# One product moved behind two others, two PSUM rings swapped, and attention steps issued earlier in a fused attention and MLP kernel

## The chip, the core and the metric

The kernel runs on one core of a Trainium2 chip. The metric is device time in microseconds of one execution. The median of three runs before the change is 495.05 us (492.89 to 496.14).

## The reference

x is 2048 x 512 (float32). It is normalised by row; from the normalised rows come a dilated local attention and an MLP that gates it.

```python
x = A_x
xn = _layernorm(x)                                    # 2048 x 512
q, k, v = split(xn @ wqkv)                            # 512 x 1536; 32 heads of 16
idx = pos[:, None] - 2 * arange(8)                    # 8 keys, 2 rows apart
logits = einsum(q, k[idx]) * 16 ** -0.5               # idx < 0: -1e9
s = einsum(softmax(logits), v[idx]) @ wo              # 512 x 512
h = relu(xn @ w1 + b1) ** 2                           # 512 x 1792
g = silu(h @ w2 + b2)                                 # 1792 x 512
out = x + s * g
```

## The kernel before, in words

**Products in three passes.** Each float32 operand is split into a rounded high part and the rest, the low part. A product runs over high x high, high x low and low x high, so a 128 x 512 result over a depth of 512 takes 12 matmuls of 128 x 512, and one over a depth of 256 takes 6. ScalarE writes high parts (`highx`, `sum_high`, `high`), VectorE or GpSimd subtract to get low parts (`lowx`, `sum_low`, `low`, `lowh`).

**Phase 1: q, k and v** (main loop from L787). The 2048 rows are 16 tiles of 128. Tiles are taken in pairs a, b = a + 1. Pairs 0 and 2 compute q, k, v with 12 matmuls each (`qkv`). The six pairs a = 4, 6, ..., 14 go through `seven(a)` (L571): with sums and differences of the two tiles and of the weights, q and k of both tiles take seven products of 6 matmuls where eight would be needed, and v two products of 12. Its work on TensorE, in the order before, for pairs 4 to 12:

1. X, first product, into a new bank X; ScalarE then copies X into a bank Y (`A.activation(Y, X, AF.Copy)`);
2. v of tile a (`qkv(a, 2)`);
3. the second product on X, after which ScalarE copies X out as q of tile a;
4. the tail product of the pair before (`last`, L647), on that pair's bank Z, after which ScalarE copies Z out as q of its tile b;
5. v of tile b;
6. a product on Y, which ScalarE copies into a bank Z; then products on U, on Z and again on Y. VectorE adds Z and Y to U's copy (the two `V.tensor_add` into `sk_`, "stg" in the trace), which gives k.

In pair 14 v of tile b stood at the end, before the tail product, and two first products of the MLP, `up(0, 0)` and `up(0, 1)`, followed.

The third and sixth matmul of a product read the low part. The products on U, Z and Y read `ss`, the sums of two tiles: `sum_x` forms them on VectorE and GpSimd one pair ahead, `sum_high` rounds them on ScalarE, and `sum_low` subtracts one half on VectorE and the other on GpSimd. Tile t + 2 is transposed by VectorE (`trans`, L474), its high part written by ScalarE and its low part by VectorE (`lowx`).

**PSUM.** Eight banks in three rings: psA with four banks (X, v of a, v of b, U), psH with two (Y and Z of a pair, later `ph`), psT with two (the transposes, later the output product). A new tile of a ring waits until the tile that had its bank has been read for the last time.

**Attention** is a generator (L239) that issues steps on VectorE: for each of eight units of 256 rows four steps q x k (a multiplication of 128 x 2048 and a reduction), the softmax, and four steps attention x v (the same two operations). They are put between the other VectorE work by `pump(margin)` (L366). It keeps two planned clocks, of TensorE and VectorE, and issues steps as long as VectorE's planned clock, with the next step's cost, stays within TensorE's planned clock plus the margin: -500 ns without an argument, `LATE` = 3000 ns, or 500. The price of a matmul is 227 ns, that of a VectorE operation its elements / 0.96 + 170 ns. `not_before` moves VectorE's clock forward where an operation must wait for another engine. Loads of q, k and v for a unit are issued from ScalarE's queue when the planned clock has passed a due time, which `defer` holds (L231).

TensorE, VectorE, ScalarE and GpSimd keep the order in which the program issues; DMAs on SP may be reordered against the program.

**Phase 2: the MLP** (from L896) runs over four chunks c of 512 rows and 14 blocks f of 128 hidden columns: `up(c, f)` (12 matmuls into `ph` of psH; ScalarE applies relu and two squares, VectorE's `lowh(f)` the low part), then `down` of block f - 2 (12 matmuls into four banks `pb` of psA). `up(c, f)` takes the bank of `up(c, f - 2)`, which is free when `lowh(f - 2)` has read it. In chunks 1 to 3 five of the fourteen low parts are on GpSimd. In chunk 0 the weights arrive: `load_w(f)` loads w1 and w2 of block f into two pieces of SBUF, `next_w()` splits them (two ScalarE operations, two on GpSimd) and, from block 3 on, issues the load of block f + 2, which waits until GpSimd has read the pieces. The output products of a chunk (`pw`) and the gate run between blocks; the last two tiles of the last chunk need the last attention step, its store to DRAM (so) and its load (oq).

Of the kernel before, what the change touches and what calls it, by code (L numbers as in the profile page):

```python
# [10 lines left out]
AF = mybir.ActivationFunctionType  # L11
# [29 lines left out]
SEVEN = range(4, 15, 2)  # L41
# [10 lines left out]
MATMUL, TRANSPOSE, DVE_FIXED, SLACK, LATE, ROOM0, ROOM = 227, 150, 170, 500, 3000, 500, 3500  # L52
# [5 lines left out]
def body(ctx: ExitStack, tc: tile.TileContext, x, wqkv, wo, w1, b1, w2, b2, out):  # L58
# [32 lines left out]
    PE, V, A, G = Ordered(nc.tensor, "PE"), Ordered(nc.vector, "V"), Ordered(nc.scalar), Ordered(nc.gpsimd)  # L91
# [15 lines left out]
    def psA(name):  # L107
        return psum.tile([P, 512], F32, name=name, tag="acc", bufs=4)

    def psH(name):  # L110
        return psum.tile([P, 512], F32, name=name, tag="h", bufs=2)
# [38 lines left out]
    def buffer(name, i):  # L150
        return wts.tile([P, 2, 2, 512], FR, name=name, tag=f"b{i}")


    wq = [buffer(f"wq{i}", i) for i in range(6)]
# [84 lines left out]
    def attention():  # L239
# [5 lines left out]
        def qk(u, s):  # L245
# [11 lines left out]
                out=L[:, i0 * 8:(i0 + 2) * 8, :].rearrange("p m w -> p w m"),  # L257
                in_=pr.rearrange("p w (g d) -> p w g d", d=HD), axis=AX.X, op=OP.add)

# [106 lines left out]
    def pump(margin=-SLACK):  # L366

        limit = clock["PE"] + margin
        flush(clock["PE"])
        while True:  # L370
            if coming[0] is None:
                coming[0] = next(stream, None)
            if coming[0] is None or clock["V"] + coming[0] > limit:
                break
            coming[0] = next(stream, None)
        if coming[0] is None:
            not_before(limit)
# [4 lines left out]
    def load_w(f):  # L382
        if f in (1, 2):
            r1, r2 = (px.tile([P, D], F32, name=f"{n}{f}", tag="x", bufs=4) for n in ("w1r", "w2r"))
        else:
            r1, r2 = (piece(f"{n}{f}") for n in ("w1r", "w2r"))
        dma(r1.rearrange("p (k c) -> p k c", c=P), w1[:, f * P:(f + 1) * P].rearrange("(k p) c -> p k c", p=P))
        dma(r2, w2[f * P:(f + 1) * P, :])
        raws[f] = r1, r2

    def next_w():

        f = len(w12)
        if f < NF:
            w12[f] = buffer(f"w{f}", HOME[f]) if f in HOME else p2.tile([P, 2, 2, 512], FR, name=f"w{f}")
            for i, r in enumerate(raws.pop(f)):
                split(w12[f][:, 0, i], w12[f][:, 1, i], r, G)
            if 2 < f < NF - 2:
                load_w(f + 2)


    NT = S // P
# [71 lines left out]
    def trans(t, aside=False):  # L474
        place(t)
        pTs[t] = piece(f"xs{t}") if t % 2 and t - 1 in SEVEN else psT(f"pxT{t}")
        if t < TURN:
            for kt in range(KT):
                PE.transpose(pTs[t][:, kt * P:(kt + 1) * P], xn[t][:, kt * P:(kt + 1) * P], ident)
            seen[t] = clock["PE"] + 800  # L480
        else:

            V.transpose(out=pTs[t].rearrange("p (k n b) -> p b k n", k=KT, b=4),
                        in_=xb[t // 2 * 2][:, :, t % 2].rearrange("p b (k c) -> p b k c", k=KT))
            seen[t] = clock["V"] + 800
        if not aside:
            highx(t)
# [4 lines left out]
    def lowx(t):  # L492
        not_before(seen.pop(t))
        V.tensor_sub(xt[t][:, 1], pTs[t].rearrange("p (k n) -> p k n", k=KT), xt[t][:, 0].bitcast(F32))
        if t not in SEVEN and t - 1 not in SEVEN:
            pTs.pop(t)
# [18 lines left out]
    def sum_high(a):  # L515
        ss[a] = [pss.tile([P, 2, 2, 2, P], FR, name=f"ss{a}_{i}", tag="ss", bufs=2) for i in range(2)]
        for t, d in zip(sums[a], ss[a]):
            A.activation(d[:, :, 0], four(t), AF.Copy)
# [7 lines left out]
    def qkv(t, s, between=None, late=False):  # L526

        ps = (psH if t < 2 and s == 2 else psA)(f"pq{t}_{s}")
        order = [(kt, a, b) for kt in range(KT) for a, b in PASSES]
        if late:  # L530
            order.sort(key=lambda o: o[1])
        for n, (kt, a, b) in enumerate(order):
            PE.matmul(ps, xt[t][:, a, kt], wq[2 * s + kt // 2][:, b, kt % 2, :], start=n == 0, stop=n == 11)
            if between and n == 5:
                between()
        evacuate(t, s, ps)
# [34 lines left out]
    def seven(a):  # L571

        b = a + 1
        for s in (2, 0, 1):
            stgs[s] = pstg.tile([P, 4, 2, P], F32, name=f"stg{a}_{s}", tag="stg", bufs=5)
        sq_, sk_ = stgs[0], stgs[1]

        def x(t, h):
            return lambda p, k: xt[t][:, p, 2 * h + k]

        def s(i):
            return lambda p, k: ss[a][i // 2][:, i % 2, p, k]

        def product(ps, left, w, start=False, stop=False):
            n = 0
            for k in range(2):
                for p, r in PASSES:
                    PE.matmul(ps, left(p, k), w[:, r, k], start=start and n == 0, stop=stop and n == 5,
                              skip_group_check=True)
                    n += 1  # L590

        def groups(ps):
            return ps.rearrange("p (g c) -> p g c", g=4)

        X = psA(f"X{a}")
        product(X, x(a, 0), wq[0], start=True)
        Y = psH(f"Y{a}")
        A.activation(Y, X, AF.Copy)
        if a == SEVEN[0]:
            sum_high(a)  # L600
        more = a + 2 < NT
        if not more:
            sum_high(a)
        first_norm(a)
        second_norm(a)
        pump(LATE)
        qkv(a, 2)
        if more and a > SEVEN[0]:
            sum_high(a)
        pump(LATE)  # L610
        product(X, x(a, 1), wq[1], stop=True)
        A.activation(sq_[:, :, 0], groups(X), AF.Copy, scale=0.25)
        while tail:
            tail.pop()()
        sum_low(a)
        if more:
            trans(a + 2)
            pump(LATE)
            qkv(b, 2)
            lowx(a + 2)  # L620
            trans(b + 2, True)
        else:
            load_w(3)
        pump(LATE)
        product(Y, s(1), tw[T2])
        Z = psH(f"Z{a}")
        A.activation(Z, Y, AF.Copy)
        if more:
            highx(b + 2)
        else:  # L630
            next_w()
        U = psA(f"U{a}")
        product(U, s(0), tw[T1], start=True, stop=True)
        A.activation(sk_[:, :, 0], groups(U), AF.Copy)
        if more:
            lowx(b + 2)
            sum_x(a + 2)
            next_stats(a)
        pump(500)
        product(Z, s(2), tw[T3])  # L640
        product(Y, s(3), wq[3], stop=True)
        pump(500)
        V.tensor_add(sk_[:, :, 1], groups(Z), sk_[:, :, 0])
        V.tensor_add(sk_[:, :, 0], groups(Y), sk_[:, :, 0])
        store(a, 1, sk_)

        def last():  # L647
            product(Z, x(b, 1), tw[T4], stop=True)
            A.activation(sq_[:, :, 1], groups(Z), AF.Copy, scale=0.25)
            store(a, 0, sq_)  # L650

        tail.append(last)
        if not more:
            pump(LATE)
            qkv(b, 2, next_w)
            load_w(4)
            tail.pop()()
            pump(LATE)
            up(0, 0)
            next_w()  # L660
            pump()
            up(0, 1)
            lowh(0)
            pump()

    def load_xT(c):
        xT[c] = xTa.tile([P, TPC, 2, KT, P], FR, name=f"xU{c}", tag="xT")
# [2 lines left out]

    hs = {}

    def up(c, f):
        ph = psH(f"ph{c}_{f}")
        n = 0
        for kt in range(KT):
            for a, b in PASSES:
                PE.matmul(ph.rearrange("p (j n) -> p j n", n=P), w12[f][:, a, 0, kt * P:(kt + 1) * P],
                          xT[c][:, :, b, kt, :], start=n == 0, stop=n == 11)
                n += 1  # L680
        if f == NF - 1 and c + 1 < NCH:
            load_xT(c + 1)
        h = hpool.tile([P, 2, 512], FR, name=f"h{c}_{f}", tag="h", bufs=3)
        A.activation(ph, ph, AF.Relu, bias=b1t[:, f:f + 1])
        A.activation(h[:, 0], ph, AF.Square)
        aside = c > 0 and f in ASIDE
        if aside:
            r, ph = ph, p2.tile([P, 512], F32, name=f"sq{c}_{f}", tag="sq", bufs=2)
        else:
            r = ph  # L690
        A.activation(ph, r, AF.Square)
        hs[f] = h, ph, clock["PE"] + 2000, aside
# [37 lines left out]
    ps = psA("pq0_1")  # L730
# [56 lines left out]
    for a in range(2, NT, 2):  # L787
        b = a + 1
# [224 lines left out]
```

## Time and profile before

| | us |
|---|---|
| median of three runs | 495.05 |
| the profiled execution | 494.42 |
| its span | 492.3 |
| TensorE busy | 481.3 |
| VectorE busy | 438.1 |
| ScalarE busy | 228.2 |
| GpSimd busy | 168.3 |

All instructions that the kernel issues through a helper have line L87, so groups are told apart by tile: X, Y, Z, U are the banks of a pair, pq is v (in pairs 0 and 2 also q and k), xt the transposed tile, ss the sums, stg a staged result, pr and pv the products of attention, ph and pb the MLP's banks, h its hidden block, w1r and w2r raw weights. A row of the timeline gives start, duration, engine, operation, tiles, count, and in brackets the idle time before it with what ended it. DVE is VectorE, ACT is ScalarE, POOL is GpSimd, SP issues most DMAs.

### The profile page before, as it was taken

The page shows a single profiled execution, that of the slowest core. Times are in us where ns is not written, and L with a number is a line of the kernel's source. Part 1 is how long each engine was busy: PE and PEld are TensorE (multiplying, and loading weights), DVE is VectorE, ACT ScalarE, POOL GpSimd, SP SyncE. Part 2 cuts the span into 40 slices and gives each one's busy share as a digit, 9 for nine tenths or more (in the row PEclk, how much of TensorE's full clock was granted, in tenths as well). Part 3 has the DMA queues.
Part 4 walks back from the last instruction along what each step waited for, and adds up shares of the span by engine and source line. Part 5 has one row for each costly group of instructions (what it writes and reads, how often), then busy time and mean ns, then how long its engine had stood idle before and what let it go on. Part 6 is the DMA issues. An engine that isn't in the chain of part 4 may idle for free.

```text
span 492.3 us, 5906 instructions
## 1 busy us (share of the span) xinstructions
PE 481.3 (98%) x2118; PEld 395.5 (80%) x2118; DVE 438.1 (89%) x374; ACT 228.2 (46%) x403; POOL 168.3 (34%) x153
## 2 busy tenths in 40 slices
PE   8999999989899999999999999999999999999996
PEld 5888788868688888888888888888888888888885
DVE  5997889899966999999999998899999989999806
ACT  5686566734355557445612333534232453433213
POOL 1326532633676869413222322151121022411100
PEclk9999999999899999999999999999999999999999
DMA  8799788796579866191627048325520872261052
GB/s 293 228 301 329 245 255 257 268 334 242 170 235 277 249 159 225 47 328 23 224 63 221 5 169 317 70 65 194 161 94 1 330 225 65 37 195 56 1 170 85
DMA packets 48520, 88.78 MB, mean 180 GB/s; under 512 B 5372, under 2 KB 32364, under 8 KB 45676
## 3 DMA queue, kind: packets, MB, share of 16 engines
q1 hardware_dynamic: 42444, 51.72, 33.5%
q10 hardware_dynamic: 4320, 33.56, 19.2%
q0 software_dynamic: 1728, 3.15, 3.9%
q8 instruction: 16, 0.26, 0.2%
q14 instruction: 12, 0.10, 0.1%
HBM read 57.94 MB, written 27.32 MB: 173 GB/s over the span
## 4 chain that ended last, share of the span: by engine, by line
PE 80%; DMA 8%; DVE 6%; ACT 2%; SPq 2%; issue 1%; POOL 0%; ACTq 0%; DVEq 0%; POOLq 0%
PE ph L87 31%; PE pb L87 29%; PE pw L87 7%; PE pq L87 6%; DMA xb<-xn 4%; PE Z L87 2%; PE X L87 2%; PE Y L87 2%; DVE pr L87 1%; DMA so<-v 1%; SPq L472 1%; PE U L87 1%; DMA sq<-stg 1%; DVE stg L87 1%; ACT xn L87 1%
## 5 line engine op out<-in xcount | busy, mean ns | idle before, releaser
L87 PE MATMUL pb<-w,h 128*128 128x512 f32 x672 | 160.6, 389 | 0.0
L87 PEld LDWEIGHTS pb<-w,h 128*128 128x128 f32 x672 | 126.2, 188 | 26.1
L87 PE MATMUL ph<-xU,w 128*128 128x512 f32 x504 | 120.6, 389 | 0.0
L87 PEld LDWEIGHTS ph<-xU,w 128*128 128x128 f32 x504 | 94.6, 188 | 19.6
L87 ACT ACTIVATE ph<-ph,b1t 128x512 f32<-128x512 f32 x56 | 36.9, 659 | 145.1 <-PE ph L87 131.5
L87 DVE TENSOR_TENSOR pv<-v,L 128x2048 f32<-128x2048 f32 x32 | 76.8, 2399 | 0.4
L87 DVE TENSOR_TENSOR pr<-k,q 128x2048 f32<-128x2048 f32 x32 | 76.7, 2395 | 0.4
L87 DVE TENSOR_REDUCE v<-pv 128x256 f32<-128x2048 f32 x32 | 73.0, 2282 | 0.7
L87 DVE TENSOR_REDUCE L<-pr 128x128 f32<-128x2048 f32 x32 | 72.9, 2278 | 0.5
L87 POOL TENSOR_TENSOR h<-sq,h 128x512 fp32r<-128x512 f32 x15 | 25.7, 1711 | 84.2 <-ACT sq L87 75.2
L87 PE MATMUL pw<-wot,oT 128*128 128x512 f32 (+1 forms) x204 | 46.1, 377 | 0.2 <-DVE oT L87 0.2
L87 DVE TENSOR_TENSOR h<-ph,h 128x512 fp32r<-128x512 f32 x41 | 28.1, 685 | 19.7 <-ACT ph L87 19.7
L87 PEld LDWEIGHTS pw<-wot,oT 128*128 128x128 f32 x204 | 36.7, 188 | 7.7 <-DVE oT L87 0.6
L87 PE MATMUL ph<-xT,w 128*128 128x512 f32 x168 | 40.2, 390 | 0.0
L87 PEld LDWEIGHTS ph<-xT,w 128*128 128x128 f32 x168 | 31.5, 188 | 6.8 <-DVE h L87 0.3
L87 ACT ACTIVATE h<-ph 128x512 fp32r<-128x512 f32 x56 | 33.6, 600 | 2.5
L87 PE MATMUL pq<-wq,xt 128*128 128x512 f32 x144 | 34.6, 389 | 0.0
L87 PEld LDWEIGHTS pq<-wq,xt 128*128 128x128 f32 x144 | 27.0, 188 | 5.6
L87 PE MATMUL pq<-wq,xT 128*128 128x512 f32 x132 | 30.8, 392 | 0.0
L87 POOL TENSOR_TENSOR w<-w1r,w 128x512 fp32r<-128x512 f32 x14 | 25.2, 1801 | 15.6 <-ACT w L87 11.5
L87 PEld LDWEIGHTS pq<-wq,xT 128*128 128x128 f32 x132 | 24.5, 188 | 5.8 <-ACT xT L87 0.7
L87 POOL TENSOR_TENSOR L<-L,mx_None 128x512 f32<-128x512 f32 x7 | 19.5, 2791 | 27.1 <-DVE mx_None L87 27.1
(103 smaller groups left out, 533.0 us busy)
## 6 DMA issues: line engine op xcount, KB each, us to landing
k<-sk ACTq DMA_DIRECT2D x8, 1408.0 KB, 6.9
v<-sv ACTq DMA_DIRECT2D x8, 1408.0 KB, 6.8
sx<-xt SPq DMA_DIRECT2D x12, 512.0 KB, 5.2
xU<-sx ACTq DMA_DIRECT2D x6, 1024.0 KB, 6.5
x<-in_A_x SPq DMA_DIRECT2D x16, 256.0 KB, 5.5
sk<-stg SPq DMA_DIRECT2D x8, 512.0 KB, 4.4
sq<-stg SPq DMA_DIRECT2D x8, 512.0 KB, 4.1
sv<-stg SPq DMA_DIRECT2D x8, 512.0 KB, 5.4
```

What stands on the lines that cost most here:

```text
L87: return tc.keep_in_program_order(f(*a, **k))
L472: dma(xb[t][32 * a:32 * a + 32].rearrange("p b e c -> p b (e c)"), src[:, a].rearrange("p e c -> p (e c)"))
```

## The change

In `seven(a)`:

- the second product on X and the copy that follows move behind v of tile b, for all six pairs. The tail product of the pair before thus comes directly behind v of tile a;
- pair 14 gets v of tile b at the same place as the others, no longer at its end;
- `lowx(a + 2)` moves behind `trans(b + 2)`;
- `sum_high` of pair 14 moves from before v of tile a to behind it;
- one `pump(LATE)` is added ahead of the second product on X; the pump ahead of the last products on Z and Y goes from 500 to `LATE`, the one ahead of VectorE's two adds from 500 to 1500;
- behind pair 14, `up(0, 0)` and `up(0, 1)` take their banks from psT, `up(0, 0)` stands ahead of the last tail product, the split of w2 and load 4 ahead of `up(0, 0)`, the split of w3 behind `up(0, 1)`, and two pumps get `LATE`.

```diff
+        more = a + 2 < NT
         X = psA(f"X{a}")
         product(X, x(a, 0), wq[0], start=True)
         Y = psH(f"Y{a}")
         A.activation(Y, X, AF.Copy)
         if a == SEVEN[0]:
             sum_high(a)
-        more = a + 2 < NT
-        if not more:
-            sum_high(a)
         first_norm(a)
         second_norm(a)
         pump(LATE)
         qkv(a, 2)
-        if more and a > SEVEN[0]:
+        if a > SEVEN[0]:
             sum_high(a)
         pump(LATE)
-        product(X, x(a, 1), wq[1], stop=True)
-        A.activation(sq_[:, :, 0], groups(X), AF.Copy, scale=0.25)
         while tail:
             tail.pop()()
         sum_low(a)
         if more:
             trans(a + 2)
-            pump(LATE)
-            qkv(b, 2)
-            lowx(a + 2)
-            trans(b + 2, True)
         else:
             load_w(3)
+        pump(LATE)
+        qkv(b, 2)
+        if more:
+            trans(b + 2, True)
+            lowx(a + 2)
+        pump(LATE)
+        product(X, x(a, 1), wq[1], stop=True)
+        A.activation(sq_[:, :, 0], groups(X), AF.Copy, scale=0.25)
         pump(LATE)
         product(Y, s(1), tw[T2])
...
-        pump(500)
+        pump(LATE)
         product(Z, s(2), tw[T3])
         product(Y, s(3), wq[3], stop=True)
-        pump(500)
+        pump(1500)
         V.tensor_add(sk_[:, :, 1], groups(Z), sk_[:, :, 0])
         V.tensor_add(sk_[:, :, 0], groups(Y), sk_[:, :, 0])
...
         if not more:
+            next_w()
+            load_w(4)
             pump(LATE)
-            qkv(b, 2, next_w)
-            load_w(4)
+            up(0, 0, psT)
             tail.pop()()
             pump(LATE)
-            up(0, 0)
+            up(0, 1, psT)
             next_w()
-            pump()
-            up(0, 1)
             lowh(0)
-            pump()
+            pump(LATE)
...
-    def up(c, f):
-        ph = psH(f"ph{c}_{f}")
+    def up(c, f, ps=psH):
+        ph = ps(f"ph{c}_{f}")
```

## The prediction

> **What bounds the kernel now.** I read the page first, then the table by stretches, then TensorE's timeline, then who waits for whom.
>
> ```profile
> span 492.3 us, 5906 instructions
> PE 481.3 (98%) x2118; PEld 395.5 (80%) x2118; DVE 438.1 (89%) x374; ACT 228.2 (46%) x403; POOL 168.3 (34%) x153
> ...
> 147.00:212.00 65.00, 65.00 (x289) 53.83 (x288) 59.53 (x41) 36.42 (x64) 46.85 (x27) 1.00 0.68 200
> 212.00:300.00 88.00, 88.00 (x390) 72.90 (x389) 86.72 (x61) 33.64 (x57) 21.03 (x12) 1.00 0.47 153
> ```
>
> TensorE is the bound, with 11 us of the span idle. In the table (columns: length, then PE, PEld, DVE, ACT, POOL busy, granted clock, DMA share, GB/s) VectorE is a close second: from 212 to 300 us it has 1.3 us left of 88. A gain in the pairs lasts only if VectorE can follow it there.
>
> ```profile
> 41.83 1.52 PE L87 MATMUL X<-wq,xt 128*128 128x512 f32 x6
> ...
> 100.86 1.52 PE L87 MATMUL X<-wq,xt 128*128 128x512 f32 x6
> ...
> 106.87 1.66 PE L87 MATMUL X<-wq,xt 128*128 128x512 f32 x6 [1.76 <-ACT Y L87]
> ...
> 124.70 0.61 PE L87 MATMUL Y<-t,ss 128*128 128x512 f32 x2
> 127.69 1.20 PE L87 MATMUL Y<-t,ss 128*128 128x512 f32 x4 [2.37 <-DVE ss L87]
> 128.72 2.52 PE L87 MATMUL U<-t,ss 128*128 128x512 f32 x6
> 131.04 2.18 PE L87 MATMUL Z<-t,ss 128*128 128x512 f32 x6
> 133.06 1.54 PE L87 MATMUL Y<-wq,ss 128*128 128x512 f32 x6
> ...
> 137.16 1.52 PE L87 MATMUL Z<-t,xt 128*128 128x512 f32 x6
> ...
> 147.01 2.72 PE pb L87 x12
> ...
> 130.00:132.00 2.00, 2.00 (x6) 1.52 (x6) 2.00 (x1) 1.34 (x4) 1.83 (x1) 0.50 0.89 317
> ```
>
> The six pairs run from 41.83 (first X) to 137.16 (last product on Z): 95.33 us. They hold 6 x 66 matmuls less the last 6, so 390; at 2.72 us for 12, these are 88.4. **6.9 us are lost in the pairs**: a wait of 1.76 in pair 12, one of 2.37 in pair 14, and behind the latter a granted clock of 0.50. There U takes 2.32 us from start to start and Z 2.02, against 1.36 for six, so 1.6 more. The rest is in small pieces.
>
> The Trainium skill, "TensorE: Matmul & The Clock Gate", Part 1, says that the array drops to half clock after an idle window of about 3.4 us, and warns of idle gaps above that. Half is what the row shows, but behind a gap of 2.37; by the page's length the lost time here would be 5.3 us instead of 6.9. The measurement decides.
>
> **The change part by part.** X2 is the second product on X.
>
> It waited for ScalarE's copy of X into Y, and that for VectorE's adds, which free Y:
>
> ```profile
> 104.66 0.68 DVE L87 TENSOR_TENSOR stg<-Z,stg 128x512 f32<-128x512 f32 x1
> ...
> 106.23 0.58 ACT L87 ACTIVATE Y<-X 128x512 f32<-128x512 f32 x1 [4.52 <-DVE stg L87]
> ...
> 125.89 1.74 DVE L87 TENSOR_TENSOR ss<-xs,ss 128x512 fp32r<-128x512 f32 x1
> ...
> 94.97 0.69 DVE L87 TENSOR_TENSOR ss<-xs,ss 128x512 fp32r<-128x512 f32 x1 [1.76 <-ACT ss L87]
> ...
> DVE xt L87 <- ACT xt L87: 6.9, 7, 2.3
> ...
> L87 DVE TENSOR_TENSOR pr<-k,q 128x2048 f32<-128x2048 f32 x32 | 76.7, 2395 | 0.4
> ...
> 143.25 0.69 DVE L87 TENSOR_TENSOR h<-ph,h 128x512 fp32r<-128x512 f32 x1 [1.91 <-ACT ph L87]
> ...
> 145.98 0.69 DVE L87 TENSOR_TENSOR h<-ph,h 128x512 fp32r<-128x512 f32 x1 [2.04 <-ACT ph L87]
> ```
>
> X2 now stands behind the tail product (1.36) and the other v product (2.72): 4.08 us more cover against a wait of 1.76. The wait goes. No work is added; X's copy into sq, its store on SP and its bank come 4.08 later, and the next X wants that bank some 7 us after. Late next is the tail product, now 1.36 earlier, which needs the add that reads Z. In pair 12 that add ends at 105.34, and the v product before the tail product would end at 100.86 + 4.08 = 104.94 (X12 starts at 100.86; X2 stood 4.08 behind it and came 1.93 later still).
>
> The wider pumps. I replayed pump's arithmetic (227 ns a matmul; elements/0.96 + 170 ns on VectorE), which gives the order of the VectorE rows of before, and then the new order. This is an order and no time. Counting halves of attention steps (a multiplication or a reduction), VectorE has issued 22 before the first `lowh` and will have issued 24; before `lowh(3)` 24 and 27; before the first chunk's `lowh(9)` 36 and 39; before the second chunk's `lowh(2)` 49 and 53; the last stands behind product 8 of the last chunk, not behind its end. A half costs 2.3 (pr: 2.395 with its overlaps). So the adds come up to one half later (2.3), and ss of pair 14 has two more halves ahead (4.6).
>
> What pays for them is idle time of VectorE: with `lowx` behind the second transpose, most of its 6.9 us of waits for ScalarE's xt (5 of them in the pairs, an estimate from seven waits, the longest 2.3), half of the 1.76 (0.9), and the 1.91 and 2.04 before the first two `lowh`. Going through VectorE's new list pair by pair with the durations of before, I get the add on Z 1 to 2 us ahead of each tail product, so 0 for that wait (bounds 0 and 2.7, in pair 12: 0.4 + 2.3). For pair 14: ss ended at 127.63; 4.6 later for the halves, 5 + 0.9 earlier for idle time, 1.0 earlier if it takes 0.69 as in pair 10 and not 1.74: 125.3. Y's product there starts at 124.7 + 2.72 (v15) less the 2.1 won in pair 12 and 0.4 in others: 124.9, and needs ss at its third matmul, 125.4. That is even, so I take 0.4 lost (0 to 1.6). `sum_high` of pair 14 behind v14's copy puts its two ScalarE operations 0.6 later; 2.72 cover that.
>
> The transposes' banks. up(0,0) stands where v15 ended before. In psH it would wait for the add on Y; psT is free since the pair's transposes were read, so nothing is lost and the last adds get 2.72 of cover. The split of w2 and load 4 move ahead of it on ACT, POOL and SP; up(0,2) needs w2 only 6.8 us later.
>
> So TensorE comes out of the pairs 6.9 - 0.4 = 6.5 us earlier, up(0,0) at 130.7.
>
> What is late next: weight 5. Its load waits until weight 3 has been split, and that split moves from before up(0,1) to behind it.
>
> ```profile
> 143.14 0.62 ACT L87 ACTIVATE w<-w1r 128x512 fp32r<-128x512 f32 x1
> ...
> L87 POOL TENSOR_TENSOR w<-w1r,w x14: 1287/1298/3347, 121.3 to 199.1; 128x512 fp32r<-128x512 f32 x14
> ...
> 145.15 0.38 SPq L387 DMA_DIRECT2D w1r<-in_B_w  x1
> ...
> 146.79 6.53 SPq L915 DMA_DIRECT2D rwo<-in_A_wo  x5
> ...
> 153.90 0.63 ACT L87 ACTIVATE w<-w1r 128x512 fp32r<-128x512 f32 x1 [4.70 <-DMA w1r<-in_B_w]
> ...
> 157.45 0.69 DVE L87 TENSOR_TENSOR h<-ph,h 128x512 fp32r<-128x512 f32 x1 [4.16 <-ACT ph L87]
> ...
> 160.45 2.88 PE L87 MATMUL ph<-xT,w 128*128 128x512 f32 x12
> ...
> DMA to landing us min/median/max: 2.9/3.8/10.4
> ...
> 156.00:158.00 2.00, 2.00 (x11) 1.65 (x10) 0.55 (x1) 1.39 (x3) 2.00 (x2) 1.00 0.99 248
> ...
> 191.95 0.68 DVE L87 TENSOR_TENSOR h<-ph,h 128x512 fp32r<-128x512 f32 x1
> ...
> 193.09 2.88 PE L87 MATMUL ph<-xT,w 128*128 128x512 f32 x12
> ...
> 234.15 0.68 DVE L87 TENSOR_TENSOR h<-ph,h 128x512 fp32r<-128x512 f32 x1
> ...
> 236.61 2.88 PE L87 MATMUL ph<-xU,w 128*128 128x512 f32 x12
> ...
> 160.00:180.00 20.00, 20.00 (x90) 16.57 (x89) 19.30 (x12) 10.08 (x19) 13.54 (x9) 1.00 0.80 211
> ```
>
> ScalarE stands at the split of w5 until its load has landed (4.70), and behind it stand the activations of up(0,3), on which `lowh(3)` waits (4.16); up(0,5) needs the bank that `lowh(3)` frees. New: up(0,1) ends at 130.7 + 2.72 + 1.36 + 2.72 = 137.5; three activations and the two of w3, some 3 us (0.6 each), then GpSimd's first subtraction, 1.3 to 3.3, of which I take the upper part since VectorE multiplies just then: the load goes out at 143.3, against 145.15. With the landing of before (153.90 - 145.15 = 8.75; a little less, 8, since in the new order k2 and q2 load while pair 14 runs, and only v1 takes their place on ACT's queue) it lands at 151.3. From landing to the end of `lowh(3)` were 158.14 - 153.90 = 4.2: now 155.5. up(0,5) could start at 160.45 - 6.5 = 153.95: **1.5 lost**, so 5.0 ahead.
>
> Then VectorE has no slack. Before, `lowh(9)` ended 0.46 ahead of up(0,11), and the second chunk's `lowh(2)` 1.78 ahead of its product 4. From `lowh(3)` on, VectorE is 158.14 - 155.5 = 2.6 earlier, wins the 0.70 idle of 160 to 180, and does one half more up to the latter place. TensorE can be ahead by 0.46 + 2.6 + 0.7 = 3.8 at the former and by 1.78 + 2.6 + 0.7 - 2.3 = **2.8 us** at the latter. Bounds: with the median landing, 3.8, `lowh(3)` ends 4.2 earlier and the whole 6.5 stand; with the longest, 10.4, 0.4 are left.
>
> The tail.
>
> ```profile
> 481.78 5.91 PE L87 MATMUL pw<-wot,oT 128*128 128x512 f32 x36 [0.21 <-DVE oT L87]
> ...
> 483.54 0.69 DVE L87 TENSOR_TENSOR z<-z,pw 128x512 f32<-128x512 f32 x1 [1.22 <-ACT z L87]
> ...
> 488.76 0.42 DVE L87 TENSOR_TENSOR z<-z,xlast 128x256 f32<-128x256 f32 x1
> ```
>
> The last attention output came 0.21 too late for the last products, held ScalarE's last activations, and let VectorE's ten last operations run back to back to 489.18, though the products end at 487.69 (+ 0.41 + 0.42). With attention 4 halves earlier both go: 0.2 + 0.6 = 0.8 (0.2 to 0.8).
>
> Sum: the profiled execution takes 494.42, its span and 2.1 around it; less 2.8 and 0.8 that is 490.8. The median of the three runs is 0.6 above the profiled one; I say 491.0.
>
> **Rivals.**
>
> Whole gain: weight 5 lands soon, and 6.5 + 0.8 give 487.1. For it: the loads of k2 and q2 leave that stretch. Against: the DMA share of 0.99 there, and v1 arrives.
>
> Slower: SP issues the loads of wo ahead of w5. Five of them held SP for 6.53 us, just behind w5. In front of it, w5 would go out at 149.8, land at 158.6, and `lowh(3)` end at 162.8: 1.78 - 4.7 + 0.7 - 2.3 = 4.5 us behind, so 498.1 with the tail, or 499.7 if the half clock adds its 1.6. It is a loss from `lowh(3)` ending at 159.1 on. For it: SP's order is not the program's, and w5 becomes ready nearer to wo; against: all but one of wo came behind w5.
>
> Nothing won: the waits only move, from X2 to the tail product (2.7 in pair 12) and to ss (1.6 in pair 14), up(0,1) and with it weight 5 come 4 later, and 0.4 or less is left beside the tail: 494. For it: the adds come later; against: the list above.
>
> **How the numbers follow.** Forecast 0.50 (487.1 to 493.2 by the landing), whole gain 0.18, nothing won 0.20, slower 0.12. 1% is about what a measurement of this kernel can tell from no change: 490.1 and 500.0. Faster: 0.18 and a third of the forecast's, 0.35. Slower: half of that rival's, 0.06. Same: 0.59. The range 487.0 to 494.8 leaves out the slower rival and the edges.
>
> **What would show it.** Right: no wait of TensorE at X or Y above 1 us and no granted clock of 0.50 before the first up; the first `ph` near 131; the stop in front of w5 on ScalarE, and a short wait before up(0,5); VectorE over 98% busy behind it; no 0.21 at the end. Wrong: TensorE waiting for stg at the tail product; w5 issued behind wo; weight 5 landing within 4 us.

## The result, and the profile after

| | before | after |
|---|---|---|
| median of six runs, us | 494.99 (492.89 to 496.14) | 489.91 (489.51 to 490.84) |
| the profiled execution | 494.42 | 489.87 |
| its span | 492.3 | 487.9 |

The ratio is 0.9904, with a 95% interval of 0.9882 to 0.9926. The forecast of 491.0 was 1.1 above the measured median.

The head of the page of the changed kernel (span, then busy time and share of each engine):

```profile
span 487.9 us, 5921 instructions
...
PE 480.0 (98%) x2118; PEld 394.6 (81%) x2118; DVE 438.0 (90%) x374; ACT 227.8 (47%) x403; POOL 173.3 (36%) x153
```

Its table by stretches, columns as before:

```profile
212.00:300.00 88.00, 87.19 (x385) 71.88 (x384) 86.47 (x62) 35.31 (x59) 21.41 (x13) 1.00 0.44 139
...
130.00:132.00 2.00, 2.00 (x11) 1.65 (x9) 1.97 (x2) 0.45 (x1) 2.00 (x2) 1.00 1.06 378
```

Its waits, TensorE's three longest behind its first matmuls, and VectorE's for xt (total, times, longest):

```profile
PE ph L87 <- POOL w L87: 0.9, 1, 0.9
PE pb L87 <- ACT pb L87: 0.8, 1, 0.8
PE pb L87 <- DVE h L87: 0.4, 1, 0.4
...
DVE xt L87 <- ACT xt L87: 2.7, 3, 1.1
```

The waits at X (1.76) and at ss (2.37) are gone, and so is the clock of 0.50 between 130 and 132. Three short waits have come in their place, all in the MLP. TensorE also has 0.8 idle between 212 and 300, where it had none.

Its timeline, TensorE first, then VectorE, GpSimd, SP and ScalarE around weight 5:

```profile
100.52 1.52 PE L87 MATMUL X<-wq,xt 128*128 128x512 f32 x6
...
125.00 1.71 PE L87 MATMUL Y<-t,ss 128*128 128x512 f32 x6
...
130.64 2.88 PE L87 MATMUL ph<-xT,w 128*128 128x512 f32 x12
...
140.48 0.61 PE L87 MATMUL pb<-w,h 128*128 128x512 f32 x2
141.53 2.60 PE L87 MATMUL pb<-w,h 128*128 128x512 f32 x10 [0.43 <-DVE h L87]
...
145.46 2.56 PE L87 MATMUL ph<-xT,w 128*128 128x512 f32 x10 [0.87 <-POOL w L87]
...
156.02 2.88 PE L87 MATMUL ph<-xT,w 128*128 128x512 f32 x12
...
225.02 3.01 PE L87 MATMUL pb<-w,h 128*128 128x512 f32 x12 [0.81 <-ACT pb L87]
...
233.31 2.88 PE L87 MATMUL ph<-xU,w 128*128 128x512 f32 x12
...
478.11 5.75 PE L87 MATMUL pw<-wot,oT 128*128 128x512 f32 x36
...
123.68 1.77 DVE L87 TENSOR_TENSOR ss<-xs,ss 128x512 fp32r<-128x512 f32 x1
...
153.70 0.69 DVE L87 TENSOR_TENSOR h<-ph,h 128x512 fp32r<-128x512 f32 x1 [3.66 <-ACT ph L87]
...
215.50 2.48 DVE L87 TENSOR_TENSOR z<-pb,b2t 128x512 f32<-128x512 f32 x4
...
141.01 1.08 POOL L87 TENSOR_TENSOR L<-L,sm_None 128x512 f32<-128x512 f32 x1 [2.44 <-DVE sm_None L87]
142.05 3.35 POOL L87 TENSOR_TENSOR w<-w1r,w 128x512 fp32r<-128x512 f32 x1
...
145.43 0.37 SPq L387 DMA_DIRECT2D w1r<-in_B_w  x1
...
150.71 0.63 ACT L87 ACTIVATE w<-w1r 128x512 fp32r<-128x512 f32 x1 [7.20 <-DMA w1r<-in_B_w]
```

The first down product of the kernel before, which the next paragraphs compare with the row at 140.48:

```profile
146.85 2.88 PE L87 MATMUL pb<-w,h 128*128 128x512 f32 x12
```

It is 146.85 - 140.48 = 6.37 earlier. Three more starts tell where the 4.4 us of span came from. up(0,5) is 160.45 - 156.02 = 4.43 earlier; the second chunk's product 4 (`ph<-xU`) 236.61 - 233.31 = 3.30; the last output products 481.78 - 478.11 = 3.67; the end 4.4. So more than six are won in the pairs, two are given back in the first chunk, one more at the start of the second, and one is won at the tail.

To compare kernels I cut TensorE's time at four marks: the start of X in pair 12, of the first down product (`pb`, 146.85 before and 140.48 after), of product 4 of the second chunk, and of the last output products. A is the end of the pairs with the first three up products, B the first chunk and the start of the second, C the rest up to the last mark. "Steps ahead" counts, in VectorE's timeline, the halves of attention steps (pr, L<-pr, pv, v<-pv) that stand before the first low part of h in the second chunk.

| kernel | median | ratio to before, 95% | A | B | C | steps ahead |
|---|---|---|---|---|---|---|
| before | 494.99 | 1 | 45.99 | 89.76 | 245.17 | 45 |
| changed | 489.91 | 0.9904 [0.9882, 0.9926] | 39.96 | 92.83 | 244.80 | 49 |
| product on X moved alone | 499.41 | 1.0127 [1.0088, 1.0167] | 45.81 | 89.76 | 252.23 | 44 |
| changed, pumps back | 490.69 | 0.9936 [0.9916, 0.9956] | 39.98 | 92.56 | 245.72 | 49 |
| changed, low part back | 494.28 | 1.0025 [1.0004, 1.0047] | 45.14 | 91.20 | 244.80 | 46 |
| changed, psH for the first up products | 496.43 | 1.0036 [1.0011, 1.0062] | 46.41 | 91.43 | 244.80 | 49 |
| changed, product on X back | 490.59 | 0.9922 [0.9897, 0.9946] | 39.92 | 92.57 | 244.81 | 49 |
| low part moved alone | 491.75 | 0.9949 [0.9929, 0.9968] | 45.88 | 89.75 | 244.80 | 46 |
| pair 14 and banks alone | 494.06 | 1.0009 [0.9993, 1.0024] | 41.97 | 94.87 | 244.80 | 46 |
| both of these | 491.0 | 0.9953 [0.9938, 0.9968] | 40.42 | 92.53 | 245.23 | 49 |
| changed, w3 ahead of up(0,1) | 489.63 | 0.9906 [0.9882, 0.993] | 39.97 | 92.60 | 244.80 | |
| changed, pb copies earlier | 490.38 | 0.9915 [0.9895, 0.9934] | 39.99 | 93.75 | 244.80 | |
| changed, these two edits | 490.75 | 0.9923 [0.9903, 0.9944] | 39.99 | 93.74 | 244.80 | |
| changed, w3 ahead of the attention steps | 487.53 | 0.9876 [0.9855, 0.9897] | 39.99 | 90.53 | 244.80 | 49 |

The kernels ran in three groups after the first comparison, each group on another chip and with the kernel before beside it, to which its ratios are taken. The kernel before took 494.12 beside the first four variants of the table; 494.89 beside the one with the product on X back, w3 ahead of up(0,1), the pb copies and these two edits; and 493.37 beside the other four. So between groups less than some 0.3% can't be told.

### The profile page after: what moved, and what is told of

The parts are those of the page before. It is cut to its first block, busy times and chain, and to the rows that moved or that the text cites. A ratio compares the mean times of both kernels' runs of the same rounds, so it can differ in the third digit from the quotient of the medians.

```text
span 487.9 us, 5921 instructions
## 1 busy us (share of the span) xinstructions
PE 480.0 (98%) x2118; PEld 394.6 (81%) x2118; DVE 438.0 (90%) x374; ACT 227.8 (47%) x403; POOL 173.3 (36%) x153
## 4 chain that ended last, share of the span: by engine, by line
PE 78%; DVE 9%; issue 6%; POOL 4%; ACT 2%; DMA 1%; ACTq 0%; DVEq 0%; POOLq 0%
PE pb L87 25%; PE ph L87 23%; PE pq L87 13%; PE pw L87 8%; PE X L87 3%; DVE L L87 3%; PE Z L87 3%; PE Y L87 3%; POOL w L87 2%; DVE v L87 2%; PE U L87 1%; DVE h L87 1%; DVE pr L87 1%; POOL ss L87 1%; DVE pv L87 1%
## 5 line engine op out<-in xcount | busy, mean ns | idle before, releaser
L87 DVE TENSOR_TENSOR pv<-v,L 128x2048 f32<-128x2048 f32 x32 | 78.4, 2449 | 1.3 <-POOL L L87 0.7
L87 POOL TENSOR_TENSOR L<-L,mx_None 128x512 f32<-128x512 f32 x7 | 17.6, 2515 | 41.6 <-DVE mx_None L87 41.6
L87 POOL TENSOR_TENSOR L<-L,sm_None 128x512 f32<-128x512 f32 x7 | 11.4, 1622 | 47.3 <-DVE sm_None L87 47.3
```

What stands on the lines that cost most here:

```text
L87: return tc.keep_in_program_order(f(*a, **k))
```

## The experiments

### Which part of the change is the gain

**The product on X moved alone.** On the kernel before (v of tile 15 moves with it, since the product stands behind it):

```diff
         qkv(a, 2)
...
-        product(X, x(a, 1), wq[1], stop=True)
-        A.activation(sq_[:, :, 0], groups(X), AF.Copy, scale=0.25)
...
         else:
             load_w(3)
+            pump(LATE)
+            qkv(b, 2)
+        product(X, x(a, 1), wq[1], stop=True)
+        A.activation(sq_[:, :, 0], groups(X), AF.Copy, scale=0.25)
         pump(LATE)
...
-            qkv(b, 2, next_w)
+            next_w()
```

> The kernel before with one thing moved: the second product on X and the copy behind it stand behind v of tile b in all six pairs, for which v of tile b of pair 14 comes forward too. Pumps, lowx, sum_high and the banks of the first up products stay. My theory: the wait at X in pair 12 goes (1.9 us) and Y of pair 14 gets 2.72 us of cover, but the last tail product then waits for VectorE's add on Z (1 to 3 us), and attention is no further ahead, so part is given back at the end: 1.5 to 3 us faster than before, ratio 0.994 to 0.997. Rival 'the move alone is the change': ratio 0.990 as the whole change. Rival 'the waits only move': ratio 0.998 to 1.002.

It took 499.41, ratio 1.0127: slower than before, so the expectation missed in sign. Its TensorE timeline:

```profile
134.65 2.92 PE L87 MATMUL Z<-t,xt 128*128 128x512 f32 x6 [2.89 <-DVE stg L87]
137.37 8.92 PE L87 MATMUL ph<-xT,w 128*128 128x512 f32 x36
...
463.68 5.49 PE L87 MATMUL ph<-xU,w 128*128 128x512 f32 x12 [3.74 <-DVE h L87]
```

The last tail product now stands close behind the products whose results VectorE adds, and waits 2.89 for that add; the six matmuls behind the wait take 137.37 - 134.65 = 2.72, as long as twelve at full clock. That eats what pair 12 and ss gave (A 45.81). The wait at X is gone here too. Attention is one half step behind the kernel before, and the last chunk pays 7.1 us (C), where an up product waits 3.74 for a low part. That the missing half step makes this wait is argued from VectorE's order, not tried.

**The pumps back** to 500, 500 and none on the changed kernel, and the added one taken out:

```diff
-        pump(LATE)
         product(X, x(a, 1), wq[1], stop=True)
...
-        pump(LATE)
+        pump(500)
         product(Z, s(2), tw[T3])
         product(Y, s(3), wq[3], stop=True)
-        pump(1500)
+        pump(500)
...
             lowh(0)
-            pump(LATE)
+            pump()
```

> The changed kernel with its pumps as they were before: no added pump, 500 and 500 in the pairs, the plain pump at the end. Replaying the planner's arithmetic gives the same lead of attention at every place from pair 14 on as the changed kernel (24 halves before the first lowh, 53 before the second chunk's lowh(2)); only in pairs 4 to 10 is it one half behind. My theory now: the pumps are not what puts attention ahead; ratio 0.988 to 0.992, as the changed kernel. Rival 'the wider pumps carry the gain': attention 3 to 4 halves (7 to 9 us) later, the wait at the end for oT back, ratio 0.995 or above.

490.69, ratio 0.9936, which lies between the theory's range (0.988 to 0.992) and the rival's (0.995 or above). The order of VectorE's steps is that of the changed kernel at every place that I counted (24 halves before the first low part of h, 27 before the fourth, 49 at the second chunk). The wider pumps are not what puts attention ahead. C is 0.9 longer, where TensorE waits 0.64 at 302.38 for a load of xU; whether the pumps caused that is open.

**The low part back** ahead of the second transpose, on the changed kernel:

```diff
+            lowx(a + 2)
             trans(b + 2, True)
-            lowx(a + 2)
```

> The changed kernel with lowx of tile a+2 ahead of the transpose of tile b+2, as before. By the planner's arithmetic attention then is 22 halves ahead at the first lowh, not 24, and 50 at the second chunk's lowh(2), not 53. My theory now: this swap is what puts attention ahead (VectorE's planned clock no longer jumps forward at lowx), and it takes VectorE's waits for xt away; undone, VectorE waits for xt 3 to 5 us more in the pairs, ss of pair 14 ends no earlier than TensorE needs it (wait of 0 to 2 us), and the end has less slack: ratio 0.991 to 0.996. Rival 'the swap only saves idle time that was idle anyway': ratio 0.988 to 0.991.

494.28, ratio 1.0025: these two swapped lines cost the whole gain, more than expected. VectorE's waits for xt and TensorE's longest two behind its first matmuls:

```profile
DVE xt L87 <- ACT xt L87: 6.6, 8, 1.8
...
PE Z L87 <- DVE stg L87: 2.4, 1, 2.4
PE Y L87 <- DVE ss L87: 1.1, 1, 1.1
```

The wait for xt is back at 6.6 (before 6.9, after 2.7), VectorE's two adds come later (136.19 against 132.81), and the tail product waits 2.4 for them, with half clock behind it. No wait at X is left, so the product's new place keeps that one away without the swap.

**The first up products in psH** again, on the changed kernel:

```diff
-            up(0, 0, psT)
+            up(0, 0)
...
-            up(0, 1, psT)
+            up(0, 1)
```

> The changed kernel with up(0,0) and up(0,1) in the banks of psH, as before. In the changed kernel's trace up(0,0) starts at 130.64 and VectorE's add on Y, which would free its bank, ends at 134.29. My theory: up(0,0) waits some 3.6 us, with 1 to 2 us of half clock behind it; the later waits of 0.4, 0.9 and 0.8 go, so 2 to 4 us slower than the changed kernel: ratio 0.994 to 0.998. Rival 'the bank does not matter, as it did not before': ratio 0.988 to 0.992.

496.43, ratio 1.0036; here too more is lost than was expected.

```profile
135.98 4.61 PE L87 MATMUL ph<-xT,w 128*128 128x512 f32 x12 [3.56 <-DVE stg L87]
140.42 1.52 PE L87 MATMUL Z<-t,xt 128*128 128x512 f32 x6
142.97 5.78 PE L87 MATMUL ph<-xT,w 128*128 128x512 f32 x24 [1.02 <-ACT stg L87]
```

up(0,0) takes Y's bank, so it waits 3.56 for the add on Y, and its twelve matmuls last 140.42 - 135.98 = 4.44 where 2.72 is the full rate. up(0,1) then waits for Z's bank. This run was also 1.65 late at X of pair 12, from the start of the kernel, which A leaves out. Attention is as far ahead as in the changed kernel (49), so the lead by itself is not the gain.

**The product on X back** at its old place, on the changed kernel:

```diff
         pump(LATE)
+        product(X, x(a, 1), wq[1], stop=True)
+        A.activation(sq_[:, :, 0], groups(X), AF.Copy, scale=0.25)
         while tail:
...
-        pump(LATE)
-        product(X, x(a, 1), wq[1], stop=True)
-        A.activation(sq_[:, :, 0], groups(X), AF.Copy, scale=0.25)
```

> The changed kernel with the second product on X back at its old place, ahead of the tail product; the low part behind the second transpose, the transposes' banks and the pumps stay. The replayed order of VectorE's work is that of the changed kernel to the last half step. Theory (the three parts work together): TensorE waits for ScalarE's copy into Y again, 1 to 3 us over the pairs: 0.5 to 2.5 us more than the changed kernel, ratio 0.991 to 0.996. Rival (the move of the product is worth nothing once the low part has moved): ratio 0.990 to 0.991 and no wait at X above 0.5.

490.59, ratio 0.9922. The theory fell: A is 39.92, as in the changed kernel, and this is all that TensorE waits at X:

```profile
PE X L87 <- ACT Y L87: 0.3, 1, 0.3
```

The wait of 1.76 in pair 12 was a wait for VectorE's adds, which free Y. With the low part behind the second transpose, VectorE is no longer late with them, and the product can stand where it stood. The ratio is in the theory's range (0.991 to 0.996), and its interval reaches into the rival's as well (0.990 to 0.991); the trace decides.

**The low part moved alone**, the same two lines swapped in the kernel before:

```diff
-            lowx(a + 2)
             trans(b + 2, True)
+            lowx(a + 2)
```

> The kernel before with one edit: the low part of tile a + 2 behind the second transpose. Theory (two parts, each of which lets the other work: the low part's new place takes VectorE's wait for xt and puts attention ahead; the transposes' banks cover the last adds): alone it keeps TensorE's wait of about 2.4 for ss in pair 14 or one for VectorE's last adds, with the half clock behind it; by the replayed order attention is one half step ahead of before: 1 to 3 us less, ratio 0.994 to 0.998. Rival (the low part's place is the whole change): ratio 0.990 to 0.992.

491.75, ratio 0.9949, as the theory had it. TensorE's timeline in pair 14:

```profile
125.75 2.07 PE L87 MATMUL Y<-t,ss 128*128 128x512 f32 x4 [2.90 <-DVE ss L87]
127.62 2.76 PE L87 MATMUL U<-t,ss 128*128 128x512 f32 x6
130.18 2.27 PE L87 MATMUL Z<-t,ss 128*128 128x512 f32 x6
```

No wait at X is left, but ss is still late: TensorE asks for it sooner, waits 2.90 and runs slowly behind it (U takes 2.56 from start to start, for 1.36). So A is as before, and what it wins it wins elsewhere: the pairs up to X of pair 12 (100.19 for 100.86), C, and behind the last mark (490.4 - 480.62 = 9.8 to the end of the span, 10.5 before).

**Pair 14 and the banks alone**, on the kernel before: v of tile 15 at the place of the other pairs, `sum_high` behind v of tile 14, and the end of pair 14 as changed. Its core:

```diff
-        if not more:
-            sum_high(a)
...
-        if more and a > SEVEN[0]:
+        if a > SEVEN[0]:
             sum_high(a)
...
         else:
             load_w(3)
+            pump(LATE)
+            qkv(b, 2)
...
-            pump(LATE)
-            qkv(b, 2, next_w)
+            next_w()
             load_w(4)
+            pump(LATE)
+            up(0, 0, psT)
...
-            up(0, 0)
+            up(0, 1, psT)
             next_w()
-            pump()
-            up(0, 1)
```

> The kernel before with pair 14 and its end alone as in the changed kernel: v of tile 15 at the place of the other pairs, the sums' rounding behind v of tile 14, the first two up products in the transposes' banks with the splits around them; the product on X, the low part and the pumps as before. Theory (two parts that need each other): the waits at X and at ss stay, VectorE's adds come late and TensorE waits for them at the tail product: ratio 0.998 to 1.004. Rival (the banks are the whole gain): 0.990 to 0.993.

494.06, ratio 1.0009: no gain. Its timeline, TensorE first, then SP, ScalarE and VectorE around weight 5:

```profile
106.86 1.66 PE L87 MATMUL X<-wq,xt 128*128 128x512 f32 x6 [1.76 <-ACT Y L87]
...
127.40 1.54 PE L87 MATMUL Y<-t,ss 128*128 128x512 f32 x6
...
145.10 2.57 PE L87 MATMUL pb<-w,h 128*128 128x512 f32 x10 [1.66 <-DVE h L87]
...
160.75 3.02 PE L87 MATMUL ph<-xT,w 128*128 128x512 f32 x12 [2.20 <-DVE h L87]
...
149.99 1.83 SPq L913 DMA_DIRECT2D rwo<-in_A_wo  x4
151.92 0.39 SPq L387 DMA_DIRECT2D w1r<-in_B_w  x1
...
156.92 0.63 ACT L87 ACTIVATE w<-w1r 128x512 fp32r<-128x512 f32 x1 [11.06 <-DMA w1r<-in_B_w]
...
160.00 0.69 DVE L87 TENSOR_TENSOR h<-ph,h 128x512 fp32r<-128x512 f32 x1 [8.24 <-ACT ph L87]
```

This is the kernel to learn from. The wait for ss and the half clock are gone, because v of tile 15 stands in front of Y's product: A is 4.0 less than before. And all of it is given back in B, which is 5.1 more, mostly at two places.

At the first down product TensorE, being earlier, waits 1.66 for the first low part of h. VectorE reaches it at 144.36, directly behind an attention step, where it was at 143.25 before.

At up(0,5) it waits 2.20, and this wait is weight 5, not attention. GpSimd has read the piece that this load needs at 142.71 + 2.87 = 145.58, but SP stands 8.0 in front of the load of b2t, until a store of q has landed, then issues four loads of wo, and weight 5 only at 151.92. ScalarE stands 11.06 for it, and VectorE 8.24 in front of the fourth low part. This is what the prediction's rival "slower" described, in a kernel with one part of the change alone.

The expectation had the waits at ss and stg staying; the first went and the second didn't come.

**Both of these together**, so the changed kernel without the product's move and without the wider pumps:

> Both of these together on the kernel before, so the changed kernel without the move of the product on X and without the wider pumps. Theory (these two parts are the gain, and together more than the sum of each alone): ratio 0.989 to 0.993. Rival (the product's move or the pumps are needed as well): 0.995 or more.

491.0 (490.18 to 493.1), ratio 0.9953: the rival's figure, beside a kernel before that was faster than in the other groups. By the marks it is nearly the changed kernel (A 40.42, B 92.53, 49 steps ahead), and its profiled span is 488.3. In A and in the steps ahead the two parts make more together than apart: A falls by 0.1 and 4.0 alone and by 5.6 together, the lead grows by 1 and 1 alone and by 4 together. In the time this can't be told: 0.9949 and 1.0009 alone, 0.9953 together. By the medians of this group the swap alone wins 1.6 us and both parts 2.4; the profiled execution of both is the fastest of its twelve and that of the swap alone lies 0.4 above its median, so the marks show the two further apart than the times do. So the theory holds for TensorE's time in the pairs and for the lead, and whether the product's move and the pumps add a last microsecond (491.0 against 489.91, in another group) stays open.

The lead is not all that the swap brings. The three kernels that have v of tile 15 at its new place but not the swap (the product moved alone, the low part back, pair 14 and banks alone) issue weight 5 at 149.53, 150.94 and 151.92. That is 5.2, 4.3 and 6.3 after GpSimd has read its piece, behind b2t and three or four loads of wo. With the swap SP issues it as soon as the piece is read (145.43 in the changed kernel, 145.70 here). The order of SP's loads thus changes with the order on VectorE, and no run here has the one without the other, so how much of the first chunk's time is the lead and how much is weight 5 stays open.

### What limits the first two chunks

**w3 ahead of up(0,1)**, on the changed kernel:

```diff
-            up(0, 1, psT)
             next_w()
+            up(0, 1, psT)
```

> The changed kernel with the split of w3 ahead of up(0,1) instead of behind it. Theory (VectorE and the second chunk's start set the end): TensorE's wait of 0.87 us for GpSimd's w3 at up(0,3) goes and weight 5 is loaded some 2 us earlier, but the wait for pb at the second chunk's first down product takes most of it back: 0 to 0.5 us less than the changed kernel, ratio 0.988 to 0.991. Rival (the weights of the first chunk set the time): the whole 1.0 to 1.5 us stay, ratio 0.987 to 0.988.

489.63, ratio 0.9906: nothing won on the changed kernel, but not for the reason expected. TensorE's wait stayed at 0.9. GpSimd's timeline shows why:

```profile
141.08 1.08 POOL L87 TENSOR_TENSOR L<-L,sm_None 128x512 f32<-128x512 f32 x1 [2.43 <-DVE sm_None L87]
142.12 3.35 POOL L87 TENSOR_TENSOR w<-w1r,w 128x512 fp32r<-128x512 f32 x1
```

ScalarE splits w3 four microseconds earlier (135.81 for 139.67), but GpSimd's half is still behind a softmax product that waits 2.43 for VectorE, since the attention steps are issued ahead of both. GpSimd keeps the program's order. The edit did not do what it said, so it tells nothing of the rival.

**The copies into pb earlier**, on the changed kernel:

```diff
+            pb = [psA(f"pb{c + 1}_{j}") for j in range(TPC)]
+            for j in range(TPC):
+                A.activation(pb[j], b2t, AF.Copy)
```

directly behind the gates, and the same lines taken out at the start of the next chunk.

> The changed kernel with ScalarE's four copies of b2t into the next chunk's pb banks issued directly behind the gates, ahead of that chunk's first two up products. Theory (ScalarE's order made pb late: an activation table load of 1.28 us and an exponential stood in front of the copies): TensorE's wait of 0.81 at the second chunk's first down product goes, with the 0.3 that follows it: 0.8 to 1.1 us less than the changed kernel, ratio 0.988 to 0.989. Rival (VectorE is the limit there, as the prediction had it): another wait takes its place, 0, ratio 0.990 to 0.991.

490.38, ratio 0.9915, next to the rival's range (0.990 to 0.991), and what the rival described. The wait at pb goes and another comes, one product sooner:

```profile
222.94 3.06 PE L87 MATMUL ph<-xU,w 128*128 128x512 f32 x12 [1.72 <-DVE h L87]
```

The copies take 2.14 of ScalarE, and the activations of the chunk's first up product, now behind them, make its low part late.

**Both edits:**

> Both of these edits on the changed kernel. Theory: w3's split earlier wins 1.0 to 1.5 us up to the second chunk and the early copies let it stay: 1.5 to 2.5 us less than the changed kernel, ratio 0.985 to 0.988. Rival (VectorE's work limits from the first chunk on): as the better of the two alone, 0.988 to 0.990.

490.75, ratio 0.9923, as the worse of the two; the theory fell with its parts, and the rival, which had the better of the two (0.988 to 0.990), fell as well.

**w3 ahead of the attention steps too**, on the changed kernel:

```diff
             tail.pop()()
+            next_w()
             pump(LATE)
             up(0, 1, psT)
-            next_w()
             lowh(0)
```

> The changed kernel with the split of w3 directly behind the last tail product, so also ahead of the attention steps that are issued before up(0,1). In the kernel that only put it ahead of up(0,1), GpSimd's half stayed where it was, behind GpSimd's softmax product, which waits 2.43 for VectorE's sum: an in-order queue. Theory: with the split ahead of that product GpSimd subtracts w3 2 to 3 us earlier, weight 5 is issued 3 to 5 us earlier, TensorE's wait of 0.9 at up(0,3) goes and ScalarE's stop in front of w5 shrinks: 0.5 to 1.5 us less than the changed kernel, ratio 0.987 to 0.989. Rival (the second chunk's start takes it back, as with the two edits before): ratio 0.990 to 0.992.

487.53 (487.23 to 488.28), ratio 0.9876. Each of its five runs is below each of the changed kernel's six (489.51 and up); the intervals of the two ratios overlap, since the kernel before was faster in this group. Its timeline, GpSimd, SP, ScalarE, VectorE and TensorE:

```profile
138.74 1.29 POOL L87 TENSOR_TENSOR w<-w1r,w 128x512 fp32r<-128x512 f32 x1
...
141.24 0.84 SPq L387 DMA_DIRECT2D w1r<-in_B_w  x1
...
146.48 0.63 ACT L87 ACTIVATE w<-w1r 128x512 fp32r<-128x512 f32 x1 [3.81 <-DMA w1r<-in_B_w]
...
150.56 0.68 DVE L87 TENSOR_TENSOR h<-ph,h 128x512 fp32r<-128x512 f32 x1
...
213.51 2.48 DVE L87 TENSOR_TENSOR z<-pb,b2t 128x512 f32<-128x512 f32 x4
...
223.05 2.88 PE L87 MATMUL pb<-w,h 128*128 128x512 f32 x12
...
231.21 2.88 PE L87 MATMUL ph<-xU,w 128*128 128x512 f32 x12
```

Weight 5 is issued 4.2 earlier (141.24 for 145.43). VectorE's stop of 3.66 in front of the fourth low part is gone, VectorE reaches the gates of the first chunk 2.0 earlier (213.51 for 215.50), and the wait at pb is gone, although ScalarE's order there was not touched. Product 4 of the second chunk starts 236.61 - 231.21 = 5.4 earlier than before. So the 0.81 at pb in the changed kernel was VectorE's lateness handed on: gates late, ScalarE's silu late (9.80 idle in front of it, ended by VectorE's z), copies late. The first theory, that ScalarE's order alone made it, does not hold: here the order is the same and the wait is gone, and with the copies earlier another wait took its place.

## Why the prediction came out as it did

**The pairs: right in time, half right in cause.** up(0,0) was said for 130.7 and started at 130.64; ss was said to end at 125.3 and ended at 125.45; 0.4 was to be lost there, and Y's product took 0.2 more than its 1.52. The waits at X and ss and the half clock behind the latter went. "X2 now stands behind the tail product and the other v product ... The wait goes" is right as it stands: with the product moved and the low part at its old place (the product moved alone, the low part back) no wait at X is left. But the move is not needed, since the swap of `lowx` and `trans` takes that wait too: with the product back it is 0.3. And without the swap the move has a price, which the sum put at 0: the last tail product then waits 2.89 or 2.37 for VectorE's adds. So the swap, which the prediction had as one payer among several, carries more than it was given. The cover of v of tile 15 for ss was right (the wait is gone in "pair 14 and banks alone" too), though 1.1 of that wait is left where the product on X has moved without the swap.

**"The wider pumps": wrong in cause.** The replayed counts were right (24, 27 and 39 halves are in the trace before the same low parts; four more than before at the second chunk). They stay when the pumps go back. The lead comes from the new place of the low part and the new end of pair 14 together: 46 with either, 49 with both. I had replayed the whole change, and not its parts. With psH for the first up products the lead is 49 as well and the time is 496.43, so the lead is not enough.

**The transposes' banks: right.** Without them up(0,0) waits 3.56 and loses 1.7 more by the clock.

**Weight 5: two errors that cancel.** Issue was said for 143.3 and came at 145.43: GpSimd's queue was taken to be free, and w3's half stood behind the softmax product (2.44 idle, then 3.35 for itself). Landing was said to take 8, and ScalarE's split began 150.71 - 145.43 = 5.28 after the issue, within the 3.8 to 10.4 that were given as bounds. The fourth low part ended at 154.4, 1.1 sooner than said, and up(0,5) waited for nothing. Not foreseen were the 0.87 and 0.43 of waits just before, at up(0,3) and the first down product; from the first down product (146.85 - 140.48 = 6.37 ahead) to up(0,5) (4.43) 1.9 are lost, near the 1.5 said, but in other places.

**VectorE as the next limit: right, the place and the form not.** "TensorE can be ahead by ... 2.8 us at the latter"; it was 3.30. That these two lie close is luck. In the changed kernel the low part that frees the bank of product 4 ends at 231.09 + 0.69 = 231.78, 3.05 earlier than before (234.83), and 1.53 ahead of the product: it did not bind. The limit did not show as a late low part but one step further on, through the gates and ScalarE to pb, and that it was VectorE is shown by the kernel with w3 first, where VectorE's stop and the wait at pb go together.

**The tail: 0.8 said, 1.1 measured** (4.4 of span less 3.30). The sum had 3.6 of span and got 4.4; against the profiled times 494.42 - 489.87 = 4.55. For the median its own terms give 490.8 + 0.6 = 491.4; the 491.0 was a choice between the two, and the measured median and profiled execution are level (489.91 and 489.87).

**The rivals.** "Slower", with the loads of wo ahead of weight 5, did not come in the changed kernel: their first issue stands at 151.60. That order did come in the three kernels with v of tile 15 moved and without the swap, where weight 5 goes out at 149.53 to 151.92, and in one of them TensorE waited 2.20 for it at up(0,5). So that it stayed away goes with the swap, which the prediction did not count for it. "Nothing won" is what the changed kernel becomes without either the swap or the banks (494.28 and 496.43), and the wait for VectorE's add that it named is the one that returns. "Whole gain" at 487.1 is what the changed kernel gives when weight 5 is issued sooner: 487.53, by an issue earlier rather than a landing faster.

## What to carry to other kernels

When two engines are nearly level, cut a change into what it does for the one and for the other, and try each alone: the new end of pair 14 won 4 us in its own stage and nothing in the end by itself; with two swapped lines on VectorE a part of it stayed. A wait named after a semaphore (X for Y's copy, pb for ScalarE's copy) is often the last link of a chain; look for the engine with no idle time behind it before moving the link. Before moving work forward, read what stands ahead of it on every in-order queue that it is issued to: w3's split moved on ScalarE and stood still on GpSimd, and in three kernels weight 5 stood 4 to 6 us on SP behind loads that the program has after it.

## What the runs showed of the hardware

**Half clock behind short stalls.** TensorE ran at half rate behind stalls of 2.37 (before, and with the low part back, where the next six matmuls took 2.34 for 1.36), 2.89 and 3.74 (product alone), 2.90 (low part alone, granted clock 0.52 from 125 to 132) and 3.56 (psH), and not behind 1.66, 1.72, 1.76 and 2.20. The Trainium skill, "TensorE: Matmul & The Clock Gate", Part 1, puts the window at about 3.4 us. These traces do not agree: the shortest stall with half clock behind it is 2.37, and the longest without is 2.20. These are single executions, so no exact length is shown.

By the mean granted clock it does not come in every execution. In the last group the kernel before ran 25 times: 13 with a mean granted clock of 0.997 or more and a median span of 490.8, 12 below that with 492.1. The changed kernel's six runs have 0.999 or 1.000. So part of the scatter of before goes with it and, as far as these means tell, part of the gain.

**GpSimd beside VectorE.** The same subtraction of 128 x 512 takes 1.29 and 3.35 (rows at 138.74 and 142.05 above). The slow ones lie beside VectorE's multiplications of 128 x 2048, which have two inputs. Two of these in the changed kernel:

```profile
134.20 3.22 DVE L87 TENSOR_TENSOR pv<-v,L 128x2048 f32<-128x2048 f32 x1
...
141.99 2.28 DVE L87 TENSOR_TENSOR pr<-k,q 128x2048 f32<-128x2048 f32 x1
...
133.99 1.29 POOL L87 TENSOR_TENSOR w<-w1r,w 128x512 fp32r<-128x512 f32 x1
```

The one that starts second is stretched. At 141.99 the multiplication is first and takes its 2.28, and the subtraction begun at 142.05 ends 1.13 behind it. At 134.20 the multiplication starts while a subtraction of 1.29 is running, and takes 3.22. The Trainium skill, "GPSIMD Engine Reference", section "1. Specifications", says that the two share their SBUF interfaces and contend when VectorE's instruction has two SBUF inputs; the trace agrees and gives the price here as 2.06 us for one subtraction.
